# Dense rows and input pairs of a recurrent-memory transformer: transposes by DMA in place of TensorE transposes

## Chip, core and metric

One core of a Trainium2 chip. The metric is the device time of one execution in microseconds (us), as the median of several runs. TensorE (PE) multiplies matrices into PSUM, VectorE (DVE) and ScalarE (ACT) copy and compute, GpSimd (POOL) does some element-wise work, and SyncE (SP) issues most of the DMA transfers, in one queue.

## What is computed

Two kinds of layers alternate, A, B, A, B, each with a layer norm ahead and a residual behind:

```python
x = x + _A_ref(_layernorm(x), ...)   # attention over 64 segments, recurrent memory
x = x + _B_ref(_layernorm(x), ...)   # relu(x @ w1) @ w2
x = x + _A_ref(_layernorm(x), ...)
x = x + _B_ref(_layernorm(x), ...)

# _A_ref: x is (1, 2048, 512); 32 heads of 128; segments of 32 rows, 8 rows of memory
for s in range(n_seg):
    xs = x[:, s * seg_len:(s + 1) * seg_len, :]
    h = jnp.concatenate([mem, xs], axis=1)             # 40 rows
    q, k, v = h @ Wq, h @ Wk, h @ Wv                   # for each head
    p = softmax(where(mask, q @ k.T * scale, -1e9))
    o = (p @ v) @ Wo                                   # summed over the heads
    mem = o[:, :M, :]                                  # the next segment's memory
    outs.append(o[:, M:, :])
```

Weights and input are bf16. The memory makes the segments of a layer sequential.

## The kernel before

All weights stay in SBUF. The work is a chain of 68 steps (NSTEP, line 55), written out by a Python loop over `step(k)` (line 691). Step k handles segment k of the first A layer and segment k - 4 of the second (DELTA, line 18) side by side, so that steps 4 to 63 are two-layer steps; the first four and the last four have one layer. `act` (line 692) lists the layers of a step.

A step goes twice over 16 heads. `qk` (half 0) projects Q and K in three batches of 6, 6 and 4 heads (24, 24 and 16 matmuls for Q, the same for K) and calls `after0(n)` behind batch n (line 731). Then come the step's values: `load_tokens0` loads the values of the segment's tokens, made earlier, from DRAM into the tile Vs (line 754), `memory_values` multiplies the memory rows by Wv, ScalarE copies the result to VmS, and a DMA stores it to DRAM (vmd, line 756); `values1` does the same for the second layer's tokens (vd, even steps, line 758). Loads bring them to Vs in the layout that the attention needs (lines 760 to 764): first those of the first half of the heads, then those of the second. The scores follow (line 765), then the exponentials (`exponents`), and `qk` (half 1) with `after1(n)` behind its batches (line 789); in its time DVE, ScalarE and GpSimd work out the softmax P of half 0. Then `transpose_p` (line 819) transposes P on TensorE, the second half's scores are made, and `weighted_v` multiplies P by Vs. The rest of the step does the same for half 1, with fills between: the feed-forward layer, the output projection, values for later steps.

Rows of the feed-forward layer B are gathered in dense tiles of 128 rows. A tile's way is `dense_moments`, `dense_normalize` (line 470, writes xn), `dense_T` (line 474, the transpose to dnT), `dense_h` (line 477, times w1 and relu on ScalarE, to hT) and `dense_y` (times w2). In the two-layer steps with k = 4m + 1 the tile `hw` is transposed right behind the scores of half 0 (line 767) and all of its `dense_h` stands in `after1(0)` (line 797). With k = 4m + 2 the tile `sooner` is transposed at the same place, and its `dense_h` is cut into three pieces behind the second half's attention (lines 841, 858 and 903). Every fourth step, k = 4m, normalises a pair of input tiles (four segments, 128 rows, `pair_normalize` in `after0(0)`) and transposes it with `pair_T` at the end of the step (line 885); its columns are read by `tokens_T` two steps later at the earliest.

`transpose_x` (line 244) is the transpose: four TensorE transposes of 128 x 128 into one PSUM tile, and a ScalarE copy (line 250 of the profile) of 128 x 512 to SBUF. xn has one buffer, shared by pairs, dense tiles and the blocks of the second layer; dnT has one, shared with the output rows `ob` that `store` writes (line 525); the pairs' xnT0 has two.

The order is the written one: `manual_schedule` (line 912) keeps the instructions of TensorE, DVE, SyncE and ScalarE in the order in which the program emits them. Only GpSimd's order is left to the scheduler.

Of the kernel before, what the change touches and what calls it, by code (L numbers as in the profile page):

```python
# [7 lines left out]
BF = mybir.dt.bfloat16  # L8
# [14 lines left out]
def kernel(  # L23
# [14 lines left out]
    nc = tc.nc  # L38
# [8 lines left out]
    NC4 = Dm // 128  # L47
# [10 lines left out]
    wk = ctx.enter_context(tc.tile_pool(name="wk", bufs=2))  # L58
# [28 lines left out]
    def one(i):  # L87

        rows = [r for r, _, _ in tenants[i]]
        return rows[0] if len(rows) == 1 else None  # L90
# [9 lines left out]
    pairs = {}  # L100
# [124 lines left out]
    dnT_tiles, wo_tiles = {}, {}  # L225
    vmds, vds = {}, {}

    def moments_of(R, r0=0, n=128):
        sl = slice(r0, r0 + n)
        stats = wk.tile([128, 6], F32, tag="ln_stats", bufs=1, name="stats")  # L230
        nc.vector.bn_stats(out=stats[sl, :], in_=R[sl, :])
        mv = wk.tile([128, 2], F32, tag="ln_mv", bufs=1, name="mv")
        nc.vector.bn_aggr(out=mv[sl, :], in_=stats[sl, :])
        rstd = wk.tile([128, 1], F32, tag="ln_rstd", bufs=1, name="rstd")
        nc.vector.tensor_scalar_add(out=rstd[sl, :], in0=mv[sl, 1:2], scalar1=LN_EPS)  # L235
        nc.gpsimd.tensor_tensor(out=rstd[sl, :], in0=rstd[sl, :], in1=mhalf_t[sl, :], op=ALU.pow)  # L236
        return sl, mv, rstd

    def normalize(out, R, m):
        sl, mv, rstd = m  # L240
        nc.vector.tensor_scalar(out=out[sl, :], in0=R[sl, :], scalar1=mv[sl, 0:1], scalar2=rstd[sl, 0:1],
                                op0=ALU.subtract, op1=ALU.mult)

    def transpose_x(xn, tag, bufs, xnT=None):
        tp = ps_fill.tile([128, NC4, 128], BF, tag="fill")
        for c4 in range(NC4):
            nc.tensor.transpose(tp[:, c4, :], xn[:, c4 * 128:(c4 + 1) * 128], ident[:])
        if xnT is None:
            xnT = wk.tile([128, NC4, 128], BF, tag=tag, bufs=bufs, name=tag)
        nc.scalar.copy(out=xnT[:, 0:NC4, :], in_=tp[:])  # L250
        return xnT

    def pair_moments(n):
        pairs["m", n] = moments_of(pairs["x", n])

    def pair_normalize(n):
        pairs["n", n] = wk.tile([128, Dm], BF, tag="xn", bufs=1, name="xn")
        normalize(pairs["n", n], pairs["x", n], pairs["m", n])  # L260

    def pair_T(n):
        pairs["T", n] = transpose_x(pairs["n", n], "xnT0", 2)

    def tokens_T(s, lo, n):

# [12 lines left out]
    def odd_moments(j):  # L279
        odd_T["m", j] = moments_of(odd_x[j])  # L280
# [43 lines left out]
    def dram_values(name, tag, bufs):  # L324
        return dram.tile([2, 4, 32, 512], BF, tag=tag, bufs=bufs, name=name)
# [12 lines left out]
    def values1(k, ii):  # L338

        if ii == 0:  # L340
            vds[1, k] = dram_values("vd1", "vd1", 2)
        HT = HTs[k % 2]
        group_values(lambda c4: HT[:, c4, 1, M:L], ii, vds[1, k], ps_fill, "fill", nc.sync)
# [121 lines left out]
    dn = {}  # L465

    def dense_moments(i):
        dn["m"] = moments_of(R_tiles[i])
# [2 lines left out]
        dn["n"] = wk.tile([128, Dm], BF, tag="xn", bufs=1, name="xn")  # L471
        normalize(dn["n"], R_tiles[i], dn["m"])

    def dense_T(i):
        dnT_tiles[i] = transpose_x(dn["n"], "dnT", 1)

    def dense_h(i, lo, hi):

        xnT = dnT_tiles[i]
        r0, r1 = (0, 128) if one(i) is None else (one(i), one(i) + 64)  # L480
        for f0 in range(4 * lo, min(4 * hi, NFC), 4):
            fcs = list(range(f0, min(NFC, f0 + 4)))
            hp = ps_fill.tile([128, 4, 128], F32, tag="fill", name="hp")
            for fi, fc in enumerate(fcs):
                fs = 128 if fc < NFC - 1 else F_LAST
                for c4 in range(NC4):
                    nc.tensor.matmul(hp[0:fs, fi, r0:r1], lhsT=w1_sb[:, c4, fc * 128:fc * 128 + fs],  # L487
                                     rhs=xnT[:, c4, r0:r1], start=(c4 == 0), stop=(c4 == NC4 - 1))
            nfull = sum(1 for fc in fcs if fc < NFC - 1)
            if nfull > 0:  # L490
                nc.scalar.activation(out=hT[:, f0:f0 + nfull, r0:r1], in_=hp[:, 0:nfull, r0:r1], func=ACTF.Relu)  # L491
            if nfull < len(fcs):
                nc.scalar.activation(out=hT[0:F_LAST, NFC - 1, r0:r1], in_=hp[0:F_LAST, nfull, r0:r1], func=ACTF.Relu)
# [91 lines left out]
    def masks(act, hf):  # L585
        for a in act:
            if hf == 0:
                nc.vector.tensor_copy(out=sp_tiles[a], in_=maskb2)
            else:
                nc.scalar.copy(out=sp_tiles[a], in_=maskb2)  # L590
# [100 lines left out]
    def step(k):  # L691
        act = [a for a in range(2) if 0 <= k - a * DELTA < NSEG]
        even = k % 2 == 0
# [8 lines left out]
        hw = dw if dw is not None and (dw % 2 == 1 or dw == 0) else None  # L702
# [4 lines left out]
        lone = k == NSTEP - 1  # L707
# [3 lines left out]
        pr = (k + 4) // 4 if k % 4 == 0 and k > 0 else (1 if k == 1 else None)  # L711
        if pr is not None and 2 * pr >= NP:
            pr = None
# [17 lines left out]
        def after0(n):  # L731
            if n == 0 and done is not None:
                add_output(done)
            if n == 0 and pr is not None:
                pair_normalize(pr)
            if n > 0:
                masks(act[n - 1:n], 0)
            if n == 1 and done is not None and not lone:
                dense_moments(done)
# [8 lines left out]
        dt = sooner if sooner is not None else hw  # L748
# [3 lines left out]
        with tc.high_priority(offset=PRIO):  # L752
            if 0 in act and k > 0:
                load_tokens0(k)
            if k > 0 and not lone:
                memory_values(k)
            if 1 in act and even and 0 in act:
                values1(k, 0)
                values1(k, 1)
            for ii in range(2):  # L760
                for a in act if k > 0 else ():
                    load(q, ii, 64 * a, M, vmds[k], a * M)
                if 1 in act:
                    load(q, ii, 64 + M, SEG, vds[1, k], 0)
            scores(qks, act)
        if dt is not None and not lone:
            dense_T(dt)
        with tc.high_priority(offset=PRIO):
            ess = exponents(act)
        if done is not None and lone:  # L770
# [13 lines left out]
        if not even:  # L784
            i = p + 2 if p % 2 else p + 4
# [3 lines left out]
        def after1(n):  # L789
            if n == 0:  # L790
                probabilities(0, ess, act[-1], k)
                if k == 0:
                    set_values(2, 0, 4)
            if n == 1 and dt is not None and lone:
                dense_T(dt)
            if n == (2 if lone else 0) and hw is not None:
                dense_h(hw, 0, 3)
            if n == 1:
                masks(act, 1)

        def within1(n):
            if k == 0 and n == 1:
                set_values(2, 4, 6)
# [77 lines left out]
            output_x(nw, *nx[2:4])  # L881
        if first:
            block_T(dw, k)
        if pr is not None:
            pair_T(pr)
        s = rider(k + 1)
        if s is not None:
# [1 line left out]
        if cont:  # L889
            with tc.high_priority(offset=PRIO):  # L890
                mt = ps_c.tile([128, NC4, 32], F32, tag="c", name="mt")
                for c4 in range(NC4):
# [4 lines left out]
                                      in_=mt[:, :, lo * M:hi * M].rearrange("p c (a m) -> p c a m", m=M))  # L897
# [14 lines left out]
    with tc.manual_schedule(engines={mybir.EngineType.PE, mybir.EngineType.DVE, mybir.EngineType.SP,  # L912
                                    mybir.EngineType.Activation}):
        mem0T = const.tile([128, NC4, M], BF)
        tp = ps_fill.tile([128, NC4, 128], BF, tag="fill", name="tp0")
        for c4 in range(NC4):
            nc.tensor.transpose(tp[:, c4, :], mem0[:, c4 * 128:(c4 + 1) * 128], ident[:])
        nc.vector.tensor_copy(out=mem0T[:], in_=tp[:, :, 0:M])
        pair_moments(0)
        pair_normalize(0)  # L920
        pair_T(0)
        odd_moments(1)
        odd_normalize(1)
        set_values(0, 0, 8)
        nc.vector.tensor_copy(out=HTms[0][:, :, 0:M], in_=mem0T[:])
        memory_values(0, nc.gpsimd)
        load_tokens0(0)
        for ii in range(2):
            load(nc.gpsimd, ii, 0, M, vmds[0], 0)
        odd_transpose(1)  # L930
        odd_moments(2)
        odd_normalize(2)
        set_values(1, 0, 8)
        odd_transpose(2)
        load_pair(1)
        for k in range(NSTEP):
            step(k)
        i = NT - 1
        output_x(i, places(i)[1][0], H)
        dense_y(i - 1, 5, NFC)  # L940
        add_output(i)
        dense_moments(i)
        dense_normalize(i)
        store(i - 1)
        again(12)
        dense_T(i)
        again(4)
        dense_h(i, 0, 3)
        dense_y(i, 0, NFC)
        store(i)  # L950
# [35 lines left out]
```

## Time and profile before

| | |
|---|---|
| median of 3 runs | 1646.51 us (1646.31 to 1649.67) |
| profiled execution | 1646.86 us |
| its span | 1644.9 us |
| granted TensorE clock | 0.999 |
| DVE, ACT, POOL busy | 65%, 54%, 16% |
| DMA queue of SyncE | 107,536 packets, 108.98 MB, 21.3% of 16 engines |
| matmuls of Q and K (line 558) | 17,408, 736.4 us |
| transposes of `transpose_x` (line 247) | 208, 20.8 us |
| copies of `transpose_x` (line 250) | 52 |

The span goes from the first to the last instruction; the execution's time holds a little around it. The profile names each group by its line and tiles: `tp<-ident,xn` writes tp from ident and xn. Names of the program: xn are normalised rows, dnT and xnT their transposes, qp the projections, sp the scores, Pf the softmax and its transpose PT, vp and VmS values on their way to DRAM, hp and hT the feed-forward layer's inner rows. PEld are weight loads, which run beside matmuls. "SPq" is SyncE's queue of DMA issues. In a time line each row gives start, duration, engine, line, operation, tiles and count; rows of one engine can overlap, since matmuls are pipelined, so the start of the next row tells what a group took.

### The profile page before, as it was taken

To read this page: it belongs to the slowest core of one execution; us is meant where nothing else is said; L and a number is where in the kernel's file an instruction comes from. 1 tells how busy PE (TensorE), PEld (TensorE's weight loads), DVE (VectorE), ACT (ScalarE), POOL (GpSimd) and SP (SyncE) were. 2 spreads that over 40 slices of the span, in tenths; PEclk is the share of its full clock that TensorE was granted. 3 is DMA by queue.
4 is the path that set the end of the run, shared out by engine and by line. 5 is a ranking of instruction groups with operands and counts; after the bars stand their busy time and mean duration, and the time that the engine had idled before them with its cause. 6 is when DMAs were issued, how large, how long until landed. Compare 5 with 4: busy or idle time off the path is not lost. (4 is left out here: it accounts for less than half of the span.)

```text
span 1644.9 us, 83757 instructions
## 1 busy us (share of the span) xinstructions
PE 1610.3 (98%) x37576; PEld 1187.3 (72%) x37576; DVE 1070.5 (65%) x2581; ACT 880.3 (54%) x2467; POOL 269.2 (16%) x516
## 2 busy tenths in 40 slices
PE   6899999999999999999999999999999999999998
PEld 3567777777777777777777777777777777767766
DVE  3456766676676667667666766766676676667654
ACT  2445555555555555555555545555555555555543
POOL 3011111111111112111111211111111111111100
PEclk9999999999999999999999999999999999999999
DMA  9722221122112221212222221121222222111111
GB/s 329 261 82 61 64 63 56 59 63 69 50 61 68 60 62 59 69 46 63 66 64 64 61 67 52 61 76 58 63 63 64 60 61 69 56 59 59 50 42 37
DMA packets 110662, 119.11 MB, mean 72 GB/s; under 512 B 13672, under 2 KB 100496, under 8 KB 109664
## 3 DMA queue, kind: packets, MB, share of 16 engines
q1 hardware_dynamic: 107536, 108.98, 21.3%
q8 instruction: 294, 4.82, 1.2%
q0 software_dynamic: 2768, 4.79, 1.1%
q14 instruction: 64, 0.52, 0.1%
HBM read 65.74 MB, written 45.61 MB: 68 GB/s over the span
## 5 line engine op out<-in xcount | busy, mean ns | idle before, releaser
L558 PE MATMUL qp<-HT,Wk_sb 128*128 128x80 bf16 (+1 forms) x8704 | 367.9, 199 | 2.1 <-DMA Wk_sb<-in_A_Wk_dram 2.0
L558 PE MATMUL qp<-HT,Wq_sb 128*128 128x80 bf16 (+1 forms) x8704 | 368.5, 199 | 1.0 <-DVE HT L896 0.6
L564 DVE CAST KT<-qp 128x480 bf16<-128x480 f32 (+3 forms) x340 | 199.5, 587 | 244.1 <-PE qp L558 240.2
L558 PEld LDWEIGHTS <-Wq_sb 128*128 128x128 bf16 x8704 | 329.5, 99 | 18.4 <-issue 9.9
L558 PEld LDWEIGHTS <-Wk_sb 128*128 128x128 bf16 x8704 | 328.5, 99 | 4.0 <-DMA Wk_sb<-in_A_Wk_dram 2.1
L562 ACT CAST QT<-qp 128x480 bf16<-128x480 f32 (+3 forms) x340 | 172.0, 506 | 211.0 <-PE qp L558 208.8
L321 ACT CAST VmS<-vp 128x512 bf16<-128x512 f32 x308 | 178.7, 591 | 135.2 <-PE vp L316 130.5
L628 POOL TENSOR_TENSOR Pf<-es,sm 128x320 bf16<-128x320 f32 x187 | 135.0, 722 | 589.4 <-ACT QT L562 166.7
L613 DVE TENSOR_REDUCE mx<-sp 128x8 f32<-128x320 f32 x256 | 114.6, 487 | 95.8 <-PE sp L598 94.5
L618 ACT ACTIVATE es<-es 128x320 f32<-128x320 f32 x256 | 109.9, 467 | 53.4 <-DVE es L616 47.3
L625 DVE TENSOR_REDUCE sm<-es 128x8 f32<-128x320 f32 x256 | 120.6, 471 | 24.0 <-ACT es L618 13.7
L316 PE MATMUL vp<-Wv_sb,HTm 128*32 128x512 bf16 x2176 | 130.0, 380 | 0.7 <-ACT HTm L898 0.6
L605 PE MATMUL sp<-Wo_sb,OTm 128*32 128x512 bf16 x2144 | 128.2, 380 | 1.4 <-DMA Wo_sb<-in_A_Wo_dram 1.4
L316 PE MATMUL vp<-Wv_sb,HT 128*32 128x512 bf16 x2048 | 127.7, 380 | 0.0
L425 PE MATMUL wox<-Wo_sb,OTx 128*128 128x512 bf16 x480 | 121.1, 380 | 0.0
L616 DVE TENSOR_TENSOR es<-sp,mx 128x320 f32<-128x320 f32 x256 | 113.5, 482 | 1.0
L683 DVE CAST OTx<-pv 128x256 bf16<-128x256 f32 (+1 forms) x256 | 85.8, 386 | 41.6 <-ACT OTm L675 41.3
L675 ACT CAST OTm<-pv 128x64 bf16<-128x64 f32 (+1 forms) x512 | 93.0, 252 | 33.0 <-PE pv L652 33.0
L236 POOL TENSOR_TENSOR rstd<-rstd,mhalf_t 128x1 f32<-128x1 f32 x84 | 46.3, 552 | 337.3 <-DVE rstd L235 330.7
L638 ACT CAST PT<-tp 128x320 bf16<-128x320 f32 x136 | 59.2, 435 | 71.3 <-PE tp L637 70.0
L683 ACT CAST OTx<-pv 128x256 bf16<-128x256 f32 (+1 forms) x256 | 78.4, 360 | 29.3 <-PE pv L652 29.3
L638 DVE CAST PT<-tp 128x320 bf16<-128x320 f32 x136 | 66.9, 492 | 37.3 <-PE tp L637 36.2
(115 smaller groups left out, 1973.2 us busy)
## 6 DMA issues: line engine op xcount, KB each, us to landing
vd<-VmS SPq DMA_DIRECT2D x172, 128.0 KB
Vs<-vd SPq DMA_DIRECT2D x172, 128.0 KB
vmd<-VmS SPq DMA_DIRECT2D x134, 128.0 KB
Vs<-vmd SPq DMA_DIRECT2D x254, 32.0 KB
Vs<-vmd SPq DMA_DIRECT2D x120, 64.0 KB
Wv_sb<-in_A_Wv_dram SPq DMA_DIRECT2D x4, 1024.0 KB
R<-in_A_x_dram POOLq DMA_DIRECT2D x32, 128.0 KB, 3.0
Wq_sb<-in_A_Wq_dram SPq DMA_DIRECT2D x4, 1024.0 KB
```

Source lines behind the costliest of these rows:

```text
L316: nc.tensor.matmul(vp[32 * j:32 * j + 32, :], lhsT=lhsT(c4), rhs=Wv_sb[:, c4, n * 512:(n + 1) * 512], start=(c4 == 0), stop=(c4 == NC4 - 1 ...
L321: nc.scalar.copy(out=VmS[:], in_=vp[:])
L425: nc.tensor.matmul(wo_tiles[i][:], lhsT=ot, rhs=Wo_sb[:, h, :], start=(n == 0), stop=(n == H - 1))
L558: nc.tensor.matmul(qp[:, hi, 0:ncol], lhsT=W_sb[:, c4, h * Dh:(h + 1) * Dh], rhs=HT[:, c4, a_lo:a_hi, :], start=(c4 == 0), stop=(c4 == NC4 ...
L562: nc.scalar.copy(out=dst[:, 0:nh, a_lo * L:a_hi * L], in_=qp[:, 0:nh, 0:ncol])
L564: nc.vector.tensor_copy(out=dst[:, 0:nh, a_lo * L:a_hi * L], in_=qp[:, 0:nh, 0:ncol])
L605: nc.tensor.matmul(wo[32 * j:32 * j + 32, :], lhsT=OTm[:, h, :], rhs=Wo_sb[:, h, :], start=(h < 4), stop=(h >= H - 4), tile_position=(0, 3 ...
L613: nc.vector.tensor_reduce(out=mxs[a][:], in_=sp_tiles[a], axis=AX.X, op=ALU.max)
L625: nc.vector.tensor_reduce(out=sm[:], in_=es[:], axis=AX.X, op=ALU.add)
L628: eng.tensor_tensor(out=P[:, :, 64 * a:64 * a + L], in0=es[:], in1=sm[:].unsqueeze(2).to_broadcast([128, 8, L]), op=ALU.mult)
L638: copy(out=PT[:, 4 * p:4 * p + 4], in_=tp[:])
L683: copy(out=ot[:, 8 * q:8 * q + 8, c:c + n], in_=pvs[q, a][:, :, L - n:L])
```

## The change

A second kind of transpose, `transpose_dma`, is one DMA on SyncE's queue that reads xn and writes the transposed tile in SBUF. It takes the place of `transpose_x` in the two-layer steps, for dense tiles and for pairs from the third on. Three places move with it: `pair_T` goes from the end of the step to `after0(0)`, right behind `pair_normalize`; `dense_T` of the odd steps goes ahead of the loads to Vs; and `dense_h` of the odd steps goes from `after1(0)` to `after1(1)`, behind the masks. Steps with one layer, the first two pairs and the last tiles keep `transpose_x`.

```diff
--- before.py
+++ after.py
@@ -252,6 +252,13 @@
 
 
 
+    def transpose_dma(xn, tag, bufs):
+        xnT = wk.tile([128, NC4, 128], BF, tag=tag, bufs=bufs, name=tag)
+        nc.sync.dma_start_transpose(out=xnT[:], in_=xn[:])
+        return xnT
+
+
+
     def pair_moments(n):
         pairs["m", n] = moments_of(pairs["x", n])
 
@@ -260,7 +267,7 @@
         normalize(pairs["n", n], pairs["x", n], pairs["m", n])
 
     def pair_T(n):
-        pairs["T", n] = transpose_x(pairs["n", n], "xnT0", 2)
+        pairs["T", n] = (transpose_x if n < 2 else transpose_dma)(pairs["n", n], "xnT0", 2)
 
     def tokens_T(s, lo, n):
 
@@ -471,8 +478,8 @@
         dn["n"] = wk.tile([128, Dm], BF, tag="xn", bufs=1, name="xn")
         normalize(dn["n"], R_tiles[i], dn["m"])
 
-    def dense_T(i):
-        dnT_tiles[i] = transpose_x(dn["n"], "dnT", 1)
+    def dense_T(i, transpose=transpose_dma):
+        dnT_tiles[i] = transpose(dn["n"], "dnT", 1)
 
     def dense_h(i, lo, hi):
 
@@ -733,6 +740,8 @@
                 add_output(done)
             if n == 0 and pr is not None:
                 pair_normalize(pr)
+                if pr > 1:
+                    pair_T(pr)
             if n > 0:
                 masks(act[n - 1:n], 0)
             if n == 1 and done is not None and not lone:
@@ -757,14 +766,16 @@
             if 1 in act and even and 0 in act:
                 values1(k, 0)
                 values1(k, 1)
+            if dt is not None and len(act) > 1 and not even:
+                dense_T(dt)
             for ii in range(2):
                 for a in act if k > 0 else ():
                     load(q, ii, 64 * a, M, vmds[k], a * M)
                 if 1 in act:
                     load(q, ii, 64 + M, SEG, vds[1, k], 0)
             scores(qks, act)
-        if dt is not None and not lone:
-            dense_T(dt)
+        if dt is not None and not lone and (even or len(act) == 1):
+            dense_T(dt, transpose_dma if len(act) > 1 else transpose_x)
         with tc.high_priority(offset=PRIO):
             ess = exponents(act)
         if done is not None and lone:
@@ -792,11 +803,11 @@
                 if k == 0:
                     set_values(2, 0, 4)
             if n == 1 and dt is not None and lone:
-                dense_T(dt)
-            if n == (2 if lone else 0) and hw is not None:
-                dense_h(hw, 0, 3)
+                dense_T(dt, transpose_x)
             if n == 1:
                 masks(act, 1)
+            if n == (2 if lone else 1 if len(act) > 1 else 0) and hw is not None:
+                dense_h(hw, 0, 3)
 
         def within1(n):
             if k == 0 and n == 1:
@@ -881,7 +892,7 @@
             output_x(nw, *nx[2:4])
         if first:
             block_T(dw, k)
-        if pr is not None:
+        if pr == 1:
             pair_T(pr)
         s = rider(k + 1)
         if s is not None:
@@ -943,7 +954,7 @@
         dense_normalize(i)
         store(i - 1)
         again(12)
-        dense_T(i)
+        dense_T(i, transpose_x)
         again(4)
         dense_h(i, 0, 3)
         dense_y(i, 0, NFC)
```

## The prediction

> **What bounds the kernel now.** I read the page's busy shares first, then the busy time of the stretch that the change touches, then TensorE's time line, step by step, and SyncE's beside it. The page says:
>
> ```profile
> span 1644.9 us, 83757 instructions
> ...
> PE 1610.3 (98%) x37576; PEld 1187.3 (72%) x37576; DVE 1070.5 (65%) x2581; ACT 880.3 (54%) x2467; POOL 269.2 (16%) x516
> ...
> PEclk9999999999999999999999999999999999999999
> ```
>
> TensorE is busy for 98% at full granted clock, every other engine has slack. The sixty two-layer steps (steps 4 to 63) run from 114.93 to about 1545 us; busy time in that stretch:
>
> ```profile
> 114.93:1545.00 1430.07, 1424.82 (x33561) 1061.95 (x33561) 967.50 (x2322) 794.12 (x2236) 242.56 (x454) 1.00 0.21 61
> ```
>
> The columns after the stretch are its length and the busy time of PE, PEld, DVE, ACT and POOL. TensorE is idle for 5.25 us of 1430. So a matmul that is taken out there shortens the run by its own issue time, as long as its removal brings no wait. The groups to be removed:
>
> ```profile
> L247 PE MATMUL tp<-ident,xn 128*128 128x128 bf16 x208 | 20.8, 223 | 3.9 <-DVE xn L241 3.9
> L250 ACT COPY dnT<-tp 128x512 bf16<-128x512 bf16 x35 | 20.5, 586 | 12.6 <-PE tp L247 12.4
> L250 ACT COPY xnT<-tp 128x512 bf16<-128x512 bf16 x16 | 9.5, 591 | 9.8 <-PE tp L247 9.8
> ```
>
> 208 matmuls are 52 transposes of four. Their mean of 223 ns is a latency; what one costs is read from the starts around it, here in step 33 (804 to 829 us), TensorE and then SyncE:
>
> ```profile
> 810.52 0.57 PE L598 MATMUL sp<-KT,QT 128*40 128x40 bf16 x32
> 811.03 0.40 PE L247 MATMUL tp<-ident,xn 128*128 128x128 bf16 x4
> 811.26 1.02 PE L558 MATMUL qp<-HT,Wq_sb 128*128 128x80 bf16 x24
> 812.12 1.03 PE L558 MATMUL qp<-HT,Wk_sb 128*128 128x80 bf16 x24
> 812.98 2.62 PE L487 MATMUL hp<-dnT,w_sb 128*128 128x128 bf16 x44
> ```
>
> ```profile
> 810.39 1.25 SPq L322 DMA_DIRECT2D vmd<-VmS  x2
> 812.11 0.91 SPq L351 DMA_DIRECT2D Vs<-vmd  x2
> 813.08 0.31 SPq L351 DMA_DIRECT2D Vs<-vd  x1
> ```
>
> The transpose takes TensorE from 811.03 to 811.26, 0.23 us. In step 35, which has none, the next projection starts 0.51 us after the scores (860.02 to 860.53); in step 34, which has one, 0.74 us after. Same difference.
>
> **What is removed.** With n the step: a dense tile is transposed at n = 5, 9, ... 61 (15 times) and n = 6, 10, ... 62 (15 times), an input pair at n = 4, 8, ... 56 (14 times; pair 1 and the tiles outside the two-layer steps stay on TensorE, 8 of the 52). That is 30 x 0.23 + 14 x 0.24 (803.20 to 803.44 in step 32) = 10.3 us of TensorE, 176 of the 208 matmuls. 44 ScalarE copies of about 0.585 us, 25.7 us, go too; ScalarE is 54% busy and TensorE almost never waits for it, so I count nothing for them. What comes next once a transpose is gone is ready. In step 32 the four matmuls behind it need wm_sb; step 34 runs them straight behind the same values (851.75, 852.72) without a wait. In step 34 the softmax chain has 0.23 us less: POOL's second product ends at 842.72 and the P transposes would start at 843.01 - 0.23 = 842.78. In step 35, with no transpose, it is 865.00 against 865.12, and TensorE doesn't wait. I count nothing, but this is the thinnest of the covers.
>
> A rule of the Trainium skill bears on the 0.23 us. "VectorE: DVE Perf Modes", section "The three transpose paths", gives 390 ns for one 128x128 bf16 transpose on TensorE, so 1.56 us for four; by that the 44 would give 68.6 us. The rows here show 0.23 for four, issued back to back, so I don't use it.
>
> **What is added.** 44 DMA transposes of 128 KB, SBUF to SBUF, on SyncE's queue. The trace has none, so two costs are bounded. *Issue on SyncE*: a plain 128 KB DMA takes 0.31 to 0.34 us; four blocks of 128 columns, each at that, 1.36. I take 1 us. *Landing*: in the lines above a 128 KB store was issued at 810.39 and the load that waits for it started at 812.11, so 1.72 us is the low end. Above: GpSimd's 128 KB loads land in 3.0 us (median), and DMAs issued in the start, when the 16 engines are full, in 6.1 to 6.5. In between I reckon from packets: the main queue's 107,536 packets took 21.3% of 16 engines' 1644.9 us, 52 ns each. 512 packets of 256 bytes (128 rows, four blocks) need 512 x 52 / 16 = 1.66 us against 0.42 for 128 packets of 1 KB: 1.72 + 1.24 = 2.97. I take 1.7 to 3.0, near 2.5.
>
> **Who waits for it.** *Steps 5, 9, ...*: SyncE is free for it at 811.64 (810.39 + 1.25); the row is normalised by 810.95. dense_h is moved behind the second batch, so it needs dnT at 811.03 + 4 x 0.86 = 814.47. The allowance is 2.83 us. At 2.5 nothing waits; at 2.97 it is 15 x 0.14 = 2.1 us. Behind it in the queue are the Vs loads, whose first had to wait till 812.11 anyway: 1 us of issue moves the first head half's last load from 813.08 to about 813.6, and its user starts at 819.22. *Steps 6, 10, ...*: it follows the last Vs load (841.90); dense_h comes at 847.20 - 0.23: 5.07 us, enough. *Steps 4, 8, ...*: it now stands early, right behind the pair's normalisation (done at 782.99), and the queue's four token loads, at 780.03 to 782.11 before, come behind it: 783.0 + 1.0 + 2.1 = 786.1, before the store that SyncE next has to issue at 786.71. The pair's first user is two steps on. Moving dense_h behind the second batch also puts ScalarE's two mask copies ahead of the relus; dense_y, their user, comes 3 us later, so nothing. The buffer xn is held until the DMA has read it; its next writer is at least 13 us off (826.04 against 812). One buffer serves dnT and the output rows; the store out of it starts at 828.07 and the next transpose at about 842.
>
> **Sum.** 1646.86 us (profiled execution; span 1644.9) - 10.3 = 1636.6. The median of the runs, 1646.51, is 0.35 lower: **1636.3 us**. About 0.2%, 3.3 us, is what a measurement of this kernel can tell from no change.
>
> **Rivals.**
> 1. *Late landing* (slower). dense_h waits in the 15 odd steps. It decides from 2.83 + 10.3 / 15 = 3.5 us: above that the kernel is slower than before. At 4.5, midway between 3.0 and 6.1, 15 x 1.67 = 25 us are lost: 1661. For it: a wait that the trace doesn't yet have, in the queue that holds the most traffic. Against it: DMA engines are busy for 0.17 of step 33. Chance 0.16. The section named above gives 1309 ns per 128x128 block by the DMA crossbar; with four blocks one after another, 5.24 us by that page, I estimate 15 x 2.41 + 15 x 0.17 lost, 1675. "Advanced Engine Details and Errata", "X-Bar Transpose (TRN2)", says instead that these DMAs are as fast as regular ones; no run here shows either yet.
> 2. *A little late*: 3.2 us, 15 x 0.37 = 5.5 lost: 1642. Chance 0.13, of which 0.08 stays over 0.2% faster.
> 3. *The softmax chain takes it back* in steps 6, 10, ...: P isn't ready, so at most 15 x 0.23 = 3.5 us come back: 1640. For it the 0.06 us of cover; against it step 35. Chance 0.07.
> 4. *SyncE is held* in steps 4, 8, ...: if one issue takes over 1.66 us, the vmd store slips, then ScalarE's fourth VmS copy (it already waits for that store, at 788.89), then the exponential, which has 1.01 us to spare. It decides from 2.66 us; at 4.2 (a Wo load's issue into full queues, 16.82 us for four) 14 x 1.54 = 21.6 lost: 1658. Chance 0.05.
> 5. *Not a crossbar move at all*, but element by element: 65,536 packets x 52 ns / 16 = 213 us a transpose, over 9 ms. Chance 0.02.
>
> The forecast itself has 0.57; its own range is 1634.5 to 1638.5 (landing 1.7 to 3.0, and a few tenths less waiting of what the 5.25 us idle hold). The range reaches up to 1652, a landing of 3.9 us, and leaves out the rest of 1, 4 and 5. Faster 0.57 + 0.08 + 0.07 = 0.72, same 0.05, slower 0.16 + 0.05 + 0.02 = 0.23.
>
> **What would show it.** TensorE's transposes down from 208 to 32, ScalarE's copies of L250's kind down by 44, TensorE's busy time down by 10 us with idle in the stretch still near 5 us; a step of the cycle of four shorter by 0.23 in three of its four. Wrong: a wait of dense_h's matmuls for the DMA in dnT (rival 1 or 2), of the P transposes for POOL in steps 6, 10, ... (3), vmd stores later than their VmS copies in steps 4, 8, ... (4). The sum would be wrong too if TensorE's idle time grew without a name.

## The result, and the profile after

The changed kernel takes **1651.32 us** (median of 20 runs, 1647.89 to 1654.68), the kernel before, in turn with it on the same chip, 1647.63 (20 runs, 1646.31 to 1651.19): a ratio of 1.002, 95% interval 1.0013 to 1.0027. It is slower by 3.7 us, where 10.3 us less were forecast. The profiled execution took 1652.01 us, 5.15 more than the one of before. Its page:

```profile
span 1650.3 us, 83508 instructions
...
PE 1603.4 (97%) x37400; PEld 1179.7 (71%) x37400; DVE 1071.8 (65%) x2581; ACT 855.3 (52%) x2423; POOL 268.9 (16%) x516
...
q1 hardware_dynamic: 131472, 114.75, 23.7%
q8 instruction: 293, 4.80, 1.3%
q0 software_dynamic: 2768, 4.79, 1.1%
q14 instruction: 66, 0.54, 0.1%
```

The last four lines are DMA queues, with packets, MB and share of 16 engines. TensorE's matmuls are 176 fewer, its busy time 6.9 us less (10 was the sign that the prediction set), ScalarE's 25.0 less; and the span is longer. So TensorE waits more. The stretch of two-layer steps, its end moved by the 4.49 us that step 64 now starts later (the columns as before: length, PE, PEld, DVE, ACT, POOL; both stretches stop 8.5 us short of step 64, which starts at 1553.47 in the kernel before):

```profile
114.93:1549.49 1434.56, 1417.37 (x33385) 1054.02 (x33385) 968.83 (x2322) 769.06 (x2193) 242.27 (x454) 1.00 0.23 65
```

1434.56 - 1417.37 is 17.2 us of idle TensorE, where 5.25 were. The waits of TensorE from 114.93 to 1550 us, in total, times, longest:

```profile
PE hp L494 <- DMA dnT<-xn: 9.1, 10, 1.7
...
PE pv L659 <- DMA Vs<-vd: 1.7, 2, 1.0
PE qp L565 <- ACT QT L569: 1.4, 1, 1.4
```

These three, 12.2 us, are new (the second had 0.2 before). `dense_h` waits for the transposed tile: rival 1. By step, the length after minus before, summed over the 15 steps of each kind from step 4 to step 63, with the 14 pairs and 30 tiles at what a step without a wait shows:

| steps | removed transposes | length changed by | lost |
|---|---|---|---|
| 4m (pairs) | 14 x 0.22 = 3.1 | -0.2 | 2.9, in steps 8, 16, 28 |
| 4m + 1 (odd tiles) | 15 x 0.21 = 3.2 | +7.9 | 11.1, in nine steps nearly all |
| 4m + 2 (even tiles) | 15 x 0.20 = 3.0 | -2.8 | 0.2 |
| 4m + 3 (none) | 0 | -0.5 | 0 |

The sum is +4.45; another 0.9 us of the span lie behind step 64. One of the nine is step 33 again, TensorE and then SyncE (start, duration):

```profile
815.03 1.03 PE L565 MATMUL qp<-HT,Wk_sb 128*128 128x80 bf16 x24
815.89 1.03 PE L565 MATMUL qp<-HT,Wq_sb 128*128 128x80 bf16 x24
816.78 1.02 PE L565 MATMUL qp<-HT,Wk_sb 128*128 128x80 bf16 x24
818.63 2.62 PE L494 MATMUL hp<-dnT,w_sb 128*128 128x128 bf16 x44 [0.83 <-DMA dnT<-xn]
```

```profile
814.87 2.47 SPq L257 DMA_TRANSPOSE dnT<-xn  x1
817.43 0.77 SPq L358 DMA_DIRECT2D Vs<-vmd  x2
```

The transpose's issue holds SyncE for 2.47 us, and the tile arrives 3.76 us after its start (814.87 to 818.63). All odd steps look alike: the transpose is issued at +7.73 us, counted from the step's first matmul (step 41: +8.29), and `dense_h` is due at +10.50, an allowance of 2.77. But in nine steps (5, 13, 21, 25, 33, 37, 45, 53, 57) `dense_h` starts 3.41 to 4.61 us after the issue, when the tile has landed, and in five others in time. Step 41 lands as fast as those, but was issued late and waits 0.25 us. The issue takes 1.20 to 1.30 us in ten steps, 2.10 to 2.47 in the other five, all of them late.

What differs? The page names a second user of the DMA engines. Queues q8 and q14 carry instructions: (4.80 + 0.54) MB for 83,508 instructions are 64 bytes each. A packet of q8 is 4.80 MB / 293 = 16.4 KB, 256 instructions, and takes 0.013 x 16 x 1650.3 / 293 = 1.2 us of one engine. TensorE's 2 x 37,400 instructions are 292 such packets, so q8 is TensorE's. A two-layer step holds some 1,110 matmuls and weight loads together (2 x 33,385 in 60 steps), so TensorE's instructions need a packet every 5.5 us, at another place of the step each time. The DMA view of +7.75 to +9.75 us (queue, packets, MB, share of 16 engines) in step 33, late:

```profile
q1 hardware_dynamic: 613, 0.25, 63.4%
q8 instruction: 1, 0.02, 5.4%
```

and in step 17, in time, where q8 has no line:

```profile
q1 hardware_dynamic: 684, 0.26, 52.5%
```

**Theory F** (fetch): a packet of instructions on one of the 16 engines holds up the transfer that is in flight, by 1 to 2 us; a transfer has landed when its last packet has. **Theory Q** (queue): a landing is late through what SyncE's queue holds around it, here through the odd place ahead of the loads to Vs. A third rival: DMA transposes themselves vary. Slices of 0.25 us (a fetch is named by the slice in which it starts) show a fetch between +7.5 and +9.0 in eight of the nine late steps; 37 doesn't fit, its fetch stands at +10.0.

The packets of the trace say how. In step 17 the transpose's 512 packets of 256 bytes run from +8.91 to +9.69. In seven late steps (5, 13, 21, 25, 33, 45, 57) all but 37 to 39 of them are through by +9.75 too. Of these few, 33 or 34, about one engine's sixteenth (512 / 16 = 32), start only when the fetch has ended, and the last ends at +10.6 to +11.3: in step 21 the fetch ends at +10.27, and they run from +10.26 to +11.10. GB/s of step 21 in 40 slices of 0.1 us from +7.75 show the last store, then the transpose (the values up to 317), then the few at 8 to 10:

```profile
GB/s 0 0 0 61 266 328 389 226 41 0 0 26 317 205 215 197 202 169 54 5 0 0 0 41 20 31 8 8 8 10 10 10 10 103 154 0 0 0 0 10
```

In step 53 the issue is held, and all 512 start after +10.0. In step 37 the data are through by +9.69; the trace has 16 updates of the semaphore that tells of the landing, fifteen come by +10.16, as in step 17, and the last at +12.29. A fetch starts there at +10.21.

### The profile page after: what moved, and what is told of

Same layout as the page of the kernel before. It is cut to its first block, busy times and chain, and to the rows that moved or that the text cites. A ratio compares the mean times of both kernels' runs of the same rounds, so it can differ in the third digit from the quotient of the medians.

```text
span 1650.3 us, 83508 instructions
## 1 busy us (share of the span) xinstructions
PE 1603.4 (97%) x37400; PEld 1179.7 (71%) x37400; DVE 1071.8 (65%) x2581; ACT 855.3 (52%) x2423; POOL 268.9 (16%) x516
## 3 DMA queue, kind: packets, MB, share of 16 engines
q1 hardware_dynamic: 131472, 114.75, 23.7%
## 5 line engine op out<-in xcount | busy, mean ns | idle before, releaser
L494 PE MATMUL hp<-dnT,w_sb 128*128 128x128 bf16 (+2 forms) x1496 | 90.2, 216 | 9.9 <-DMA dnT<-xn 9.1
L494 PEld LDWEIGHTS <-w_sb 128*128 128x128 bf16 (+1 forms) x1496 | 82.7, 100 | 19.5 <-issue 16.8
```

## The experiments

Lengths of steps and their sums are differences from the profiled execution of before (1646.86 us), of one profiled execution of each kernel. Its time is the highest of its kernel's for `even_only`, `odd_only`, `late_h` and `pad`, and the lowest for `before_pad`, `combo`, `even_pad` and `even_pairlate`, so what single steps lose there need not be what they lose in the median. Edits are shown against the kernel before in the first three, else against the changed kernel; `...` marks lines left out. Each set ran beside the kernel before on one chip: its medians there were 1646.65 us for the first four, 1646.36 for `pad`, `before_pad`, `combo` and `stopwatch`, 1646.81 for the last four.

**even_only**: the even dense tiles alone by DMA, all else as before.

```diff
-            dense_T(dt)
+            dense_T(dt, transpose_dma if len(act) > 1 and even else transpose_x)
```

> Only the 15 dense tiles of steps 6, 10, ... 62 go by DMA; odd tiles and pairs as before. Theory F: a transpose lands late where an instruction fetch (a 16 KB packet on one of the 16 DMA engines) falls into its time, and nothing here waits for a landing below 5 us, so each of these steps is 0.20 to 0.23 us shorter: 3.0 to 3.5 us below the kernel before, no wait of dense_h. Theory Q: a landing is late through what SyncE's queue holds around it (stores to DRAM ahead, loads behind); the allowance of 5 us covers that too: the same 3.0 to 3.5 us.

Measured: 1648.37 us (10 runs, 1644.21 to 1651.16), ratio 1.0006 (0.9996 to 1.0016), no difference that can be told, where both theories had 3.0 to 3.5 us less. In the profiled execution (1651.16) twelve of the 15 even steps are 0.20 us shorter and `dense_h` never waits for the tile. But steps 23 and 55 are 1.65 and 3.52 us longer, step 56 1.33, and none of these has a transpose by DMA. SyncE in step 51, as before, and in step 55:

```profile
1245.58 1.20 SPq L329 DMA_DIRECT2D vmd<-VmS  x2
1247.30 0.62 SPq L358 DMA_DIRECT2D Vs<-vmd  x2
```

```profile
1341.99 1.20 SPq L329 DMA_DIRECT2D vmd<-VmS  x2
1346.00 0.63 SPq L358 DMA_DIRECT2D Vs<-vmd  x2
```

The load that waits for the plain store starts 1.72 us after the store's issue in step 51 (the figure that the prediction took for a store) and 4.01 us in step 55. The DMA view of +6.0 to +8.5 us of step 55 has a line that step 51 hasn't:

```profile
q8 instruction: 1, 0.02, 4.0%
```

So what is late need not be a transpose. By Theory F an operation that was always there is hit, since the removed instructions moved the fetches: in the profile of before, none of the 30 steps 4m and 4m + 3 has a fetch at +6.75 to +7.5, where 23 (+7.25) and 55 (+7.5) have theirs now.

**pair_only**: the pairs alone by DMA, behind `pair_normalize`.

```diff
+                if pr > 1:
+                    pair_T(pr)
...
-            dense_T(dt)
+            dense_T(dt, transpose_x)
```

> Only the 14 input pairs go by DMA, ahead of the token loads; dense tiles as before. Theory F: most of these steps are 0.22 us shorter, and a few, those with an instruction fetch beside the transpose, lose 0.5 to 1.4 us through late loads to Vs or late VmS copies; sum between -3 and +2 us. Theory Q: the token loads and stores behind the transpose come later in every such step alike, so the steps lose or gain alike, by the same amount in all 14.

Measured: 1645.21 us (10 runs), ratio 0.9989 (0.9979 to 0.9998). Ten pair steps are 0.17 to 0.23 us shorter (step 44 0.38), steps 24, 32 and 56 longer by 0.48, 0.49 and 1.02. Pairs by DMA gain about 1.4 us. Theory Q needed the same change in all 14; the three that lose have a fetch at +7.25, +8.0 and +7.5.

**odd_only**: the odd tiles alone by DMA, with the new places of `dense_T` and `dense_h`.

```diff
+            if dt is not None and len(act) > 1 and not even:
+                dense_T(dt)
...
-            if n == (2 if lone else 0) and hw is not None:
+            if n == (2 if lone else 1 if len(act) > 1 else 0) and hw is not None:
```

> Only the 15 dense tiles of steps 5, 9, ... 61 go by DMA, with dense_h behind the second batch. Both theories: these steps lose about 8 us in sum (they lost 7.9 in the changed kernel), so the kernel is 6 to 10 us slower than before. Theory F: on-time and late steps lie apart (no wait, or 0.4 to 1.8 us), and it is not the same steps as in the changed kernel, since there are other numbers of instructions ahead of each; in the late ones an instruction fetch lies between 7.5 and 9.0 us from the step's start. Theory Q: the same steps, or late by about the same in each.

Measured: 1654.28 us (4 runs), ratio 1.0041 (1.0026 to 1.0056). The odd steps are 5.85 us longer in sum, 9 of them wait for dnT (7.4 us), and step 23 loses 3.49 by a late store. Most of the loss sits in the odd tiles, but not in the same steps as in the changed kernel: 9, 29 and 41 land late here and not there, 25 the reverse; 13 and 53 waited 1.65 and 0.79 us there and wait 0.1 here. So it isn't a matter of the step.

**late_h**: the changed kernel with `dense_h` of the odd steps behind the third batch, an allowance of 3.92 us (+7.72 to +11.64).

```diff
-            if n == (2 if lone else 1 if len(act) > 1 else 0) and hw is not None:
+            if n == (2 if lone or len(act) > 1 else 0) and hw is not None:
```

> The changed kernel with dense_h of the odd steps behind the third batch of the second half, 1.15 us later, so that the allowance is 4.0 us in place of 2.83. Both theories: landings of 3.4 to 4.6 us leave waits of at most 0.6 us in some four steps, 2 us in sum in place of 10.6. The odd steps then gain about 1.5 us in place of losing 7.9, and the kernel comes to 1640 to 1643 us, 4 to 7 us below the kernel before.

Measured: **1642.71 us** (10 runs), ratio 0.9973 (0.9963 to 0.9982). `dense_h` waits 0.7 us in all, in three steps, by the profile's count of waits. 1.15 us more of allowance turn 3.7 us lost into 3.9 gained: the wait was most of the loss. The odd steps are 0.4 us shorter in sum, where 1.5 were expected. Step 7 loses 2.38 us by a late store (fetch at +7.5), step 16 1.11 as in the changed kernel.

**pad**: the changed kernel with 64 matmuls into a PSUM tile that nothing reads, ahead of the first step. They and their weight loads are 128 instructions, half a packet, so that each later packet begins half a packet earlier in the program, and its fetch comes some 2.5 us earlier in its step.

```diff
+        again(64)
```

> The changed kernel with 64 more matmuls (128 TensorE instructions, half of a 256-instruction fetch) between the prologue and step 0; the steps themselves are unchanged. Theory F (fetches of TensorE's instructions collide with the transposes): each fetch comes about 2.5 us earlier in its step, so the late odd steps become others: 9, 17, 29, 37, 49 and 61, whose fetch lay 10.0 to 10.75 us into the step, get it at 7.5 to 8.25 and wait for dnT; 5, 13, 21, 25, 33, 45, 53 and 57, whose fetch lay at 7.5 to 8.75, get it at 5 to 6.25 and wait for nothing or less. Theory Q (the queue's own traffic): the pattern stays as it was, 5, 13, 21, 25, 33, 37, 45, 53 and 57 late, since no step's transfers change. Total: 0 to 8 us for the matmuls, otherwise 3 us either way of the changed kernel.

Measured: 1659.44 us (4 runs), ratio 1.0081 (1.0066 to 1.0096); the prologue takes 7.7 us more. The late steps changed: of Theory F's 14 forecasts twelve came true, 9, 17, 29, 37, 49, 61 late and 5, 13, 21, 33, 45, 57 in time (49 and 61 late by only 0.30 and 0.14 us); 25 and 53 were late against the forecast, and 41, for which there was none, too. By Theory Q the nine late steps would have stayed; six of them are in time. Steps 25 and 53 have their fetch at +9.75 and +9.5, later than I had counted as harmful. Step 33, late in the changed kernel, has no q8 line from +7.75 to +9.75 here, and TensorE goes on without a wait:

```profile
824.34 1.02 PE L565 MATMUL qp<-HT,Wk_sb 128*128 128x80 bf16 x24
825.20 1.67 PE L494 MATMUL hp<-dnT,w_sb 128*128 128x128 bf16 x27
```

The changed kernel and `pad` together, with the fetch's place read from the slices (the upper end, +9.75, was set after steps 25 and 53 were seen):

| fetch of the step | steps | `dense_h` starts |
|---|---|---|
| at +7.5 to +9.75 | 17 | all later than +10.50, by 0.14 to 1.65 us |
| elsewhere | 13 | 10 at +10.49 or +10.50, two at +10.69 and +10.75; step 37 of the changed kernel at +12.33 |

What moved was the instruction stream, not the order of any transfer. Steps 11 and 51 lose 3.5 and 3.7 us by late stores here, and nothing in the kernel without the 64.

**before_pad**: the same 64 matmuls in the kernel before.

> The kernel before with the same 64 matmuls ahead of step 0: a control, with no DMA transpose. Theory F: the fetches move in the steps of this kernel too, and where one falls on the vmd stores (6.4 to 8 us into a step) the loads to Vs come late, so single steps lose 0.2 to 3.5 us that did not before; the time moves by 0 to 5 us over what the matmuls cost (0 to 8 us, mostly beside the prologue's loads). Theory Q: no step changes by more than 0.1 us; only the prologue does.

Measured: 1651.09 us (6 runs, up to 1655.08), ratio 1.0034 (1.0023 to 1.0046). In the profiled execution, the lowest (1650.40), 4.3 us are in the prologue and no step changed by more than 0.30. The losses in single steps that I expected are not there: of the 30 steps 4m and 4m + 3 only step 4 has a fetch at +6.75 to +7.5, and it loses nothing. By step this is nearer to what Theory Q expected; with a single fetch in that place the run doesn't tell the two apart. No trace shows where the higher times come from.

**combo**: `late_h`, with the pairs' transposes behind the scores of half 0 in place of `after0(0)`.

```diff
-                if pr > 1:
-                    pair_T(pr)
...
+        if pr is not None and pr > 1:
+            pair_T(pr)
```

> The changed kernel with dense_h of the odd steps behind the third batch, and with the pairs' transposes behind the loads to Vs and the scores of their step in place of ahead of the token loads. Both theories: odd steps near -0.1 to -0.2 us each as in the run that only moved dense_h, pair steps -0.22 each without the losses of 0.5 to 1.2 us in two or three of them (those came of loads and stores held behind the transpose), even steps -0.2. Sum -7 to -9 us, less what fetches cost in steps without a transpose (0 to 4 us): 1637 to 1643 us, 2 us or so below the run that only moved dense_h.

Measured: **1642.46 us** (10 runs), ratio 0.9977 (0.9967 to 0.9987), the same as `late_h` within the intervals, where 2 us less were expected. Its profiled execution (1639.71) is the nearest to what was forecast: 6.5 us less from step 4 to step 64, pair steps -3.0 in sum, odd ones -1.0, even ones -2.0.

**stopwatch**: `dense_h` back behind the first batch, so that it always waits and each landing can be read.

```diff
-            if n == (2 if lone else 1 if len(act) > 1 else 0) and hw is not None:
+            if n == (2 if lone else 0) and hw is not None:
```

> The changed kernel with dense_h of the odd steps back behind the first batch, where it waits in every one of them: the start of dense_h less the issue of the transpose gives each landing. Theory F: two groups, 2.0 to 2.8 us without a fetch between 7 and 9 us into the step, 3.4 to 4.7 with one; the 15 waits sum to 25 to 35 us (allowance 1.1 us), and the kernel takes 1665 to 1675 us. Theory Q: one group, 2.5 to 3.5 us, whatever the fetch.

Measured: 1679.37 us (one run), over the expected range; the odd steps lose 33.9 us. Step 17, in time, and step 21, late:

```profile
438.44 1.21 SPq L257 DMA_TRANSPOSE dnT<-xn  x1
...
534.58 1.21 SPq L257 DMA_TRANSPOSE dnT<-xn  x1
```

```profile
440.90 2.00 PE L494 MATMUL hp<-dnT,w_sb 128*128 128x128 bf16 x33 [1.26 <-DMA dnT<-xn]
...
538.62 0.54 PE L494 MATMUL hp<-dnT,w_sb 128*128 128x128 bf16 x4 [2.84 <-DMA dnT<-xn]
```

2.46 and 4.04 us. The 15 landings are two groups: 2.45 to 2.53 in 9, 17, 29, 37, 41, 61, and 3.15 to 4.04 in the nine others. Eight of the nine have a fetch at +7.75 to +9.0, none of the six has. The ninth, step 49 (3.19), has a packet of the other instruction queue. The DMA view of +7.75 to +9.25 us there:

```profile
q14 instruction: 1, 0.01, 1.3%
```

It starts at +8.71, and 32 of the 512 packets of the transpose end late, at +10.15.

**stopwatch_plain**: the same with a plain copy in place of each transpose.

```diff
-        nc.sync.dma_start_transpose(out=xnT[:], in_=xn[:])
+        nc.sync.dma_start(out=xnT[:].rearrange("p a b -> p (a b)"), in_=xn[:])
```

> Stopwatch kernel (dense_h behind the first batch) with a plain DMA of the same 128 KB, SBUF to SBUF, in place of every DMA transpose. It leaves out that dense rows and pairs are transposed. Theory F (a packet of instructions on one of the 16 DMA engines holds up any DMA in flight): two groups again, steps without a fetch at +7.0 to +9.0 us into the step on time, steps with one about 1 us later or more. Issue 0.31 to 0.34 us in place of 1.2, so landing about 1.5 to 1.9 us on time, 2.5 to 3.5 late. Rival (the crossbar form itself is what varies): one group of landings, all within 0.3 us, near 1.7, whatever is fetched. Either way the time is 1645 to 1665.

Measured: 1670.72 us (one run), over the expected range. The landings of the plain copy are two groups too: 1.99 to 2.05 us in 9, 17, 21, 29, 37, 41, 61, with 2.36 in 49, and 2.93 to 3.99 in 5, 13, 25, 33, 45, 53, 57. All seven late ones have a fetch at +7.5 to +8.75, none of the eight others has one that starts from +7.0 to +9.0 (step 49 has a packet of q14 at +8.25). Step 21, late in `stopwatch`, has its fetch at +9.25 here, when a copy has landed. So the crossbar form isn't what varies; that rival falls. In time, a transpose lands 0.45 us later than a plain copy.

**even_pad**: `even_only` with the 64 matmuls.

> The kernel with the 15 even dense tiles alone by DMA, and 64 matmuls on TensorE ahead of the first step, so that every later instruction of TensorE is fetched 64 places on. Theory F: the prologue costs 4 to 8 us; the even steps keep their 0.20 us less; the waits for vd in steps 23 and 55 (1.65 and 3.52 us without the matmuls) go, since their fetch leaves +6.4 to +8.0 us of the step, and other steps of the kind 4m + 3 with a fetch there get one. Rival (these waits belong to the steps, or to what the DMA transposes do to the queue): 23 and 55 wait again. Time 1649 to 1656.

Measured: 1656.46 us (4 runs), ratio 1.0055 (1.0040 to 1.0070), a little over the expected range. In its profiled execution (1652.12, the lowest) the waits of steps 23 and 55 are gone, as F has it, with the fetches now at +9.0 and +9.25; the prologue costs 6.5 us, 13 even steps are 0.19 to 0.21 shorter. No step 4m + 3 got a wait in their place; step 4 lost 0.98. This sets the lowest time of one kernel beside the highest of the other, so it shows that wait and fetch go together, not what the shift is worth. Where the other three runs took 4 to 6 us more, no trace shows.

**combo_pad**: `combo` with the 64 matmuls.

> The kernel with dense_h behind the third batch and the pairs' transposes behind the loads of the values, and the 64 matmuls ahead of the first step. Theory F: prologue plus 4 to 8 us; the odd steps stay without a wait for dnT, since 4.0 us of allowance covers a landing that was hit too (3.2 to 4.0), or lose some tenths in one or two; steps of the kind 4m + 3 may lose 1 to 4 us where a fetch now meets the vd store. Time 1645 to 1652, 3 to 9 above the same kernel without the matmuls. Rival (dense_h's place was lucky in the run without them): waits for dnT in four steps or more, over 1655.

Measured: 1655.70 us (4 runs), ratio 1.0052 (1.0036 to 1.0069), 13 us above `combo` where 3 to 9 were expected (by the profiles the prologue takes 6.4 us more). The time is over the 1655 of the rival, but not by its waits: the odd steps stay without a wait worth naming (the second line), as F has it; the loss is in the plain stores (the first):

```profile
PE pv L659 <- DMA Vs<-vd: 6.2, 6, 2.0
...
PE hp L494 <- DMA dnT<-xn: 0.2, 1, 0.2
```

Steps 31 (+3.62 us), 51 (+1.71), 42 (+1.60) and 54 (+0.94) lose most, all with a fetch at +7.25 or +7.5.

**even_pairlate**: even tiles and pairs by DMA, the pairs as in `combo`, odd tiles on TensorE.

> Even dense tiles and pairs by DMA, the pairs' transposes behind the loads of the values; odd dense tiles on TensorE, as before. By the removed matmuls 15 x 0.20 + 14 x 0.22 = 6.1 us less: 1640.5. Theory F: minus what fetches take in steps 4m + 3, 0 to 5 us: 1640 to 1646. If the odd tiles by DMA are worth their 15 x 0.2 when dense_h stands late enough, this is up to 3 us above the kernel that has all three (1642.46); if DMA transposes in odd steps cost more than they save even so, it is below it.

Measured: **1641.66 us** (7 runs), ratio 0.9973 (0.9962 to 0.9984). From step 4 to step 64 it takes 6.1 us less, as worked out, and no step is longer by over 0.2. Odd tiles by DMA add nothing to it that can be told, even with a late `dense_h` (1642.46 for `combo`).

## Why the prediction was wrong, step by step

**What bounds the kernel, what is removed**: right. TensorE is the bound, and a transpose that goes without a wait shortens its step by 0.20 to 0.22 us (0.23 and 0.24 taken): 9.2 us over the 44. Nothing was lost with the ScalarE copies or the thin cover of the softmax chain: even steps are 0.20 shorter in the changed kernel, so rival 3 didn't come.

**Issue on SyncE**, 1 us taken, bounds 0.31 to 1.36: 1.20 to 1.30 in most, a little over what I took; 2.10 to 2.47 in five odd steps and 1.80 to 2.20 in six even ones, outside the bounds. In the pair steps the longest was 1.87 us, in step 16, over the 1.66 from which rival 4 has the vmd store slip. That step lost 1.37 us, with ScalarE's VmS copy waiting 2.97 us for the vmd store. But rival 4 loses time only from 2.66 us on, and step 48, with an issue of 1.82, lost nothing; in step 16 a fetch (at +9.2) stands beside the stores too, and the next two took 3.88 us to issue. It is one step of 14, not 14 steps. Steps 8 and 28 lost 0.9 and 0.7 us with a fetch (+6.75 and +7.0 us) at the vmd store.

**Landing, "I take 1.7 to 3.0, near 2.5"**: this is the step that failed. 2.5 is what an undisturbed landing takes (2.45 to 2.53 in `stopwatch`), and 2.77 of allowance covers it. In part that was luck: 2.97 came of 1.66 us for 512 packets, which take 0.78 (step 17), and the issue takes 1.20, where the store's took 0.34. But I took one value for all 15 landings, and so no wait, where nine of 15 took 3.41 to 4.61 us. Against rival 1 I set that the DMA engines are busy for 0.17 of step 33, a share averaged over 16 engines and 24 us. That says how much room there is, not how long the last packets of one transfer wait behind a 16 KB packet: in step 21 that was until +11.10, where +9.69 is usual. The page of before had the q8 line (294 packets); I didn't read it.

**Rival 1, "decides from 3.5 us"**: this is what came, though by a tail and not by a later landing of all, and smaller than its price of 25 us. It decides where the 15 odd steps lose 10.3 / 15 = 0.69 us each on average; they lost 11.1 / 15 = 0.74. With the 2.9 us of pair steps, 14.2 were lost against 9.2 gained, which is the 4.45 (with the -0.5 of steps 4m + 3). The range reached up to 1652 for this rival's sake, and 1651.32 lies below that; the mechanism of the forecast did not come.

**The edits taken for nothing**: one is missing. Taking 24 instructions out of each cycle of four steps (three transposes of four matmuls and four weight loads) moves every later fetch. Steps that the change doesn't touch have transfers that TensorE waits for if they are 2 us late, and the shift puts fetches on some of them: the profiled execution of `even_only` lost 6.5 us in steps 23, 55 and 56, where 15 transposes gain 3.0. My sum treated the other steps as fixed.

**Rival 5**: no; a transpose adds 544 packets to the queue ((131,472 - 107,536) / 44), the 512 worked out and 32 more (in step 17, of 4 bytes).

The Trainium skill's "VectorE: DVE Perf Modes", section "The three transpose paths", has 1309 ns for one block by the DMA crossbar and 390 ns on TensorE; the runs show 2.5 us for a DMA of four blocks, issue and all, and 0.20 to 0.22 us of TensorE for four. "Advanced Engine Details and Errata", section "X-Bar Transpose (TRN2)", has such DMAs as fast as regular ones; 2.46 against 2.01 us in step 17 of the two stopwatches nearly agrees.

**What stays open.** Why a packet of 1.2 us costs a transfer up to 2.3 us. Where data were held in the changed kernel they end 0.9 to 1.6 us later than usual; the largest delays, the store of 4.01 us and step 37, where one update alone is 2.1 us late, are more than that. Step 37 of the changed kernel and 45 of `odd_only` have no fetch in the window; in both, fifteen of the 16 updates of the landing come in time and one after 12 us, with a fetch at +10.2, but steps 9 and 29 have one at +10.0 and lose nothing. Not every fetch there hits a store: step 11 of `combo_pad` has one at +7.25 and loses 0.17 us. And the higher times of `before_pad` and `even_pad` have no trace. No experiment took the fetches away; they were only moved.

## What to carry to other kernels

When a wait for a DMA takes the place of work on the bounding engine, give it the slow landing and not the undisturbed one: here the undisturbed took 2.5 us, and of the two allowances tried, 2.77 and 3.92, the second made the change pay. In a kernel of this length every added or removed instruction of TensorE moves the instruction fetches, and so changes which transfers elsewhere are late; a gain of 0.2 us per step is smaller than one such hit, so compare step by step and try a shift of the stream. Move off TensorE what has slack behind it (even tiles, 5 us; pairs, two steps), and leave the rest: that gave the 1641.66 us. Moving the odd tiles too, with a late `dense_h`, made no difference that can be told (1642.46).

## What the runs showed of the hardware

Instructions come by the same 16 DMA engines as data, in packets of 256, 1.1 to 1.2 us each, and a 128 KB transfer that meets one can land up to 2.3 us later (plain copy 2.01 against 2.93 to 3.99; store 1.72 against 4.01). What waits is about one engine's share, 33 or 34 of 512 packets in seven late steps. An 8 KB packet of the other engines' instructions (q14) can do it too, to a lesser degree (3.19 against 2.5 us in step 49 of `stopwatch`, 2.36 against 2.0 for the copy). Met early (in the changed kernel, `pad` and `stopwatch` a fetch at +7.5 to +8.25, in all but step 57), it stretches the transpose's issue on SyncE as well, from 1.2 to between 1.5 and 2.6 us.

The data of a DMA transpose of 128 x 512 take about 0.8 us. GB/s of step 17 in 40 slices of 0.05 us from +7.75, in the changed kernel (first the last store, then the transpose):

```profile
GB/s 0 0 0 0 0 0 0 102 205 328 328 328 369 328 348 185 82 21 0 0 0 0 0 46 97 184 236 189 256 189 215 246 195 215 220 174 97 47 16 0
```

and in `stopwatch_plain` (the store, then the copy, then the loads):

```profile
GB/s 0 0 0 0 0 0 0 102 225 307 328 328 348 348 328 226 62 21 0 0 0 0 143 287 348 348 348 389 348 226 144 41 82 102 61 123 103 102 103 41
```

The transpose moves at some 215 GB/s, the copy at some 350. The rest of the 2.5 us is issue (1.20, against 0.47 for the copy) and what lies between the data's end and the reader's start.
